# One PSUM tile of eight named banks instead of rings of PSUM tiles

## The chip, the core and the metric

The kernel runs on one core of a Trainium2 chip. A core has five engines that run their own instruction streams: TensorE (PE, matmuls; PEld is its weight load), VectorE (DVE), ScalarE (ACT), GpSimd (POOL) and SyncE (SP), and 16 DMA engines. PE writes its products to PSUM, which has eight banks of 128 partitions x 2 KB; ACT and DVE read them from there. Each engine executes its own stream in order, and an instruction that needs another engine's result waits on a semaphore. The metric is the device time in microseconds (us) of one execution; lower is better.

## The reference

Three stages are chained: causal attention over 2 x 12 heads of 448 rows and 64 columns, and two feed-forward layers on the 896 x 768 result.

```python
scores = scale * q @ k.T ; mask above the diagonal ; attn = softmax(scores) ; x = attn @ v
h = x @ w_in1 ; g = h * cos(h)                                        # 896x768 @ 768x2048
x = g @ w_out1                                                        # 896x2048 @ 2048x768
h = x @ w_in2 ; g = where(h >= 1, h, where(h <= -1, 0, (h + 1)**2 / 4))
out = g @ w_out2
```

## The kernel before

Every float32 operand of a feed-forward product is split into a high and a low part, and a product is three matmuls per chunk of 128: high x high, high x low, low x high. PE therefore has most of the work. The kernel has five parts, one behind the other on PE.

- **Attention** (to 82.6 us in the profile), in the order of the table `STEPS`: S makes scores, M their maxima, E the exponentials, T transposes, C copies them, V multiplies with v, X and Y split the result. Two-bank PSUM tiles come from the pool `ps_s` (two buffers) and one-bank tiles from `ps_t` (four).
- **Stage 1**, `stage_in_plain` (to 200 us): 16 columns blocks of the first hidden layer, each with the gate `h * cos(h)`.
- **Stage 2**, `stage_out(0)` (to 304 us): the first output product as seven products of half-sized matrices instead of eight, four steps t of each (28 in all), and three row blocks d = 0, 1, 2 in each step. A product of one step and one d is six matmuls (L1019). The sums of several of the seven products grow in the same bank (`CHAIN`): ACT or DVE reads the bank between two of them (`keep`, L1045; `result`, L1058 and L1062) and PE goes on adding to it. In the last two steps of some of the seven products the order on PE is: d = 0 of step t-1 and of t, then d = 1 of both, then d = 2 of both.
- **Stage 3**, `stage_in_split` (to 419 us): eight groups g of two hidden blocks. Groups 0 to 5 have seven products of nine matmuls each (L1283), numbered 1 to 7; groups 6 and 7 have plain products (L1382). A group runs 1, then 4 and 3 of the group before, then 6, 2, 7, 5 (group 0: 1, 5, 6, 2, 7). Products 1, 6, 7 and 4 grow in bank x, 2 in bank z, 5 and 3 in bank y. After 1, 6 and 7 ACT copies bank x to SBUF (`keep`, L1295); after 2 DVE makes the result C11 from bank z (L711), after 5 C22 from bank y. Product 7 adds to the bank that the copy behind product 6 reads, so that it has to wait for this copy; this copy is called K6 here.
- **Stage 4**, `stage_out(1)`: as stage 2, for the second layer; `result` also stores to `out`.

In stages 1 to 4 all PSUM tiles hold two banks, [128, 2, 512], from a ring of four (`new_ps`, called by `bank_of` when a name is used first). x and z of a group are the two banks of one tile (`xz`), y has the first bank of another. In stages 2 and 4, d = 0 and d = 1 of a chain are the two banks of one tile (`xa`, `za`, `va`), and the d = 2 of two chains share a tile (`xb`, `zb`).

The order of stages 1 to 4 on each engine is found by a planner (`Plan`, `Steps`). Each step is a `plan.op` with a cost, the parts of buffers that it reads and those that it writes. The planner walks the steps through a model of the engines 300 times with random changes and keeps the best order; PE's own order is fixed by that of the `plan.op` calls. `plan.buf` says which slot a buffer takes; when a slot is taken again, the first writer of each part waits in the plan for all uses of the buffer before. Inside a buffer the planner counts each bank as a part of its own. The semaphores in the program are not the planner's: the tile framework sets them as the instructions are emitted, from the tiles that they read and write.

Of the kernel before, what the change touches and what calls it, by code (L numbers as in the profile page):

```python
# [31 lines left out]

STEPS = """
# [11 lines left out]
Cz10 NbP11 Tx10 Cz9 V9 Cw10 Y8 NcP11 Cy10 Cx10 NaP11 Tz11 Tx11 Tw11 Cz11 V10 D2 Cx11 Cw11 X9 Cy11 V11 Y9 D2 F0 F1 F2 F3  # L45
# [233 lines left out]
def attention_then_two_ffn(  # L279
# [109 lines left out]
    class Pair:  # L389
# [23 lines left out]
        def S(self, g):  # L413


            n = self.n
            if g == "c":
                two = (self, pairs[n + 1])
                for pair in two:
                    pair.s["c"] = ps_t.tile([P, 512], F32, tag="t", name=f"sc{pair.n}")  # L420
# [87 lines left out]
        def T(self, g):  # L508

            n, p = self.n, self.p  # L510
            if g == "x":
                t = ps_s.tile([P, 2, 512], F32, tag="s", name=f"tx{n}")
                moves = [(t[:, j, i * QB : (i + 1) * QB], p[i][:, j, :QB]) for j in range(2) for i in range(FULL)]
                moves += [(t[:, j, 3 * QB :], p[2][:, j, 2 * QB :]) for j in range(2)]
            else:
                t = ps_t.tile([P, 512], F32, tag="t", name=f"t{g}{n}")
# [71 lines left out]
    def ffn_in_part(u, x, b, chunks):  # L588

        if u not in parts:  # L590
            parts[u] = (new_ps(), ready[u], set())
        ps, w, done = parts[u]
        s = slice(b * S, (b + 1) * S)
        for c in chunks:
# [3 lines left out]
            for n, (a, t) in enumerate(((0, 0), (0, 1), (1, 0))):  # L598
                nc.tensor.matmul(  # L599
                    ps[:, b, :S], w[:, a, c * P : (c + 1) * P], x[c][:, t, s],  # L600
# [4 lines left out]
    ps_s = ctx.enter_context(tc.tile_pool(name="ps_s", bufs=2, space=PSUM))  # L605
    ps_m = [ps_s, ps_s]
    made = []

    def new_ps():
        made.append(None)  # L610
        return ps_m[(len(made) - 1) % 4].tile([P, 2, 512], F32, tag="s", name=f"m{len(made)}")

    with ExitStack() as attn:
# [3 lines left out]
        ps_t = attn.enter_context(tc.tile_pool(name="ps_t", bufs=4, space=PSUM))  # L617
# [4 lines left out]
        warm = ps_t.tile([P, 512], F32, tag="t", name="warm")  # L622
# [38 lines left out]
    ps_2 = ctx.enter_context(tc.tile_pool(name="ps_2", bufs=2, space=PSUM))  # L661
    ps_m += [ps_2, ps_2]
# [25 lines left out]
    banks_made = [0]  # L688
# [149 lines left out]
    def stage_in_plain():  # L838

        for u in range(2):  # L840
            ps, w, done = parts[u]
            given(f"w{u}", f"w{u}", w, LETTERS)
            bank_buf(f"h{u}", (0, 1))
            things[f"h{u}"] = ps
# [17 lines left out]
        def batch(f, b, chunks):  # L862
            products(f, tile_of_bank(f)[:, b, :S], slice(b * S, (b + 1) * S), chunks, None, chunks[-1])

        def tile_of_bank(f):
            return bank_of(f"h{f}")

        def flat_products(f, s, chunks):
            products(f, flat(tile_of_bank(f))[:, s], s, chunks, 0, KD - 1)

        def gate(f):
# [6 lines left out]
            hp = [(f"h{f}", 0), (f"h{f}", 1)]  # L878

            def h():  # L880
                ps = tile_of_bank(f)
# [37 lines left out]
        for f in range(0, KF, 2):  # L919
            for u in (f, f + 1):  # L920
# [4 lines left out]
                if u >= 2:  # L925
# [8 lines left out]
                    bank_buf(f"h{u}")  # L934
            if f == 0:
                for u in (0, 1):
                    done = parts[u][2]
                    for b in range(B):
                        left = [c for c in range(KD) if (b, c) not in done]
                        if left:  # L940
                            plan.op(
                                f"P{u}.{b}", "PE", ACC * len(left), partial(batch, u, b, left),
                                [(f"w{u}", p) for p in LETTERS] + [(f"x1{c}", 0) for c in left], [(f"h{u}", b)],
                            )
            else:
                order = list(spans)
                spans.reverse()
                for n, s in enumerate(order):
                    us = KD * 3 * (0.2267 if s.stop - s.start == 512 else 0.1733)
                    half = spans_of.index(s)  # L950
                    for u in (f, f + 1):
# [3 lines left out]
                        for chunks in sets:  # L955
                            plan.op(
                                f"P{u}.{n}.{chunks[-1]}", "PE", us * len(chunks) / KD, partial(flat_products, u, s, chunks),
                                [(f"w{u}", p) for p in LETTERS] + [(f"x1{c}", 0) for c in chunks], [(f"h{u}", half)],
# [5 lines left out]

    def bank(k, name):
        t, i = BANKS[name]
        return bank_of(f"{t}{k}")[:, i, :S]

    BANKS = {
# [3 lines left out]
    }  # L973
# [6 lines left out]
    def stage_out(k, first_products=None, at_split=None, at_result=None):  # L980

        def bank_access(name):
            t, i = BANKS[name]
            return (f"{t}{k}", i)

        def split(t):
# [46 lines left out]
        def keep(name, d):  # L1033
# [3 lines left out]
            if k and name != "p1":  # L1037
                combine(
                    f"{k}{name}.{d}", "DVE", 0.62, lambda: tile_of(kept)[:, d], lambda: bank(k, f"v{d}"),
                    lambda: tile_of("p11")[:, d], ALU.add, [bank_access(f"v{d}"), ("p11", d)], [(kept, d)],  # L1040
# [5 lines left out]
                [bank_access(f"x{d}")], [(kept, d)],  # L1046
            )

        def result(name, d, m, b, chain, old):
# [4 lines left out]
            def make():  # L1054
# [13 lines left out]
                f"{k}{name}.{d}", "DVE", 0.62, make, [bank_access(f"{chain}{d}"), (f"{old}{k}", d)], [(c, d)],  # L1068
# [9 lines left out]
        for t in range(NT7):  # L1078
            p, j = SEQ[k][t]
            if t == 0:  # L1080
                bank_buf(f"xa{k}")
                bank_buf(f"xb{k}")
            if k and (p, j) == (1, 0):
                bank_buf(f"va{k}")
            if t == 2 * NJ:
                bank_buf(f"za{k}")
                bank_buf(f"zb{k}")
# [131 lines left out]
    def group(g):  # L1219
# [37 lines left out]
        def where(n):  # L1257
            return {"x": (f"xz{g}", 0), "z": (f"xz{g}", 1), "y": (f"y{g}", 0)}[PLACE[n]]

        def at(n):  # L1260
            t, s = where(n)
            return bank_of(t)[:, s, :S]

        def product(n):
            if n == 1:
                bank_buf(f"xz{g}")
                bank_buf(f"y{g}")
# [79 lines left out]
        def before(n):  # L1347
# [12 lines left out]
            "C12": ("y", 0, (("w0", 1, "R12"), ("w0", 0, "R22"))), "C11": ("xz", 0, (("w0", 1, "R11"), ("w0", 0, "R21"))),  # L1360
            "C21": ("y", 1, (("w2", 1, "R11"), ("w2", 0, "R21"))), "C22": ("xz", 1, (("w2", 0, "R22"), ("w2", 1, "R12"))),
        }

        def plain_product(name, n):
            if (name, n) == ("C12", 0):
                bank_buf(f"y{g}")
                bank_buf(f"xz{g}")
# [123 lines left out]
```

## Time and profile before

| | |
|---|---|
| median of 3 runs | 528.31 us (528.11 to 528.72) |
| the profiled execution | 528.35 us, of which the span of its instructions is 526.4 us |
| PE busy | 509.2 us, 97% |
| DVE busy | 383.9 us, 73% |
| ACT busy | 344.3 us, 65% |
| POOL busy | 96.2 us, 18% |
| PE's granted clock, mean of the span | 1.00 of full speed |
| last matmul of the span ends | 522.9 us |

Times in the rows are microseconds from the start of the span. A row of a timeline gives the start, the busy time, engine, line, operation, what is written and read, and in brackets the idle time of the engine just before it with what ended it. Matmuls overlap: one of 448 columns starts 0.20 us behind the last and is shown as busy for 0.37, so that what a product takes is read from its start to the start of the next.

### The profile page before, as it was taken

The numbers are of one execution on the slowest core, as the hardware profiler recorded it, in microseconds if no ns is written. First come the engines' busy times: TensorE is split into PE (matmuls) and PEld (weight loads), VectorE is DVE, ScalarE is ACT, GpSimd is POOL, SyncE is SP. The second block draws the span as 40 slices with busy tenths as digits, with TensorE's granted clock in tenths as the row PEclk, the third lists the DMA queues.
The fourth block names the chain that finished last, engine by engine and source line by source line (L and its number), as shares of the span: only waits on it lengthen the run. The fifth ranks groups of instructions, "written<-read, shape, count | busy, mean of one in ns | idle before, by whom it ended". The sixth has DMA issues, their size and how long they took to land.

```text
span 526.4 us, 7606 instructions
## 1 busy us (share of the span) xinstructions
PE 509.2 (97%) x2810; PEld 442.4 (84%) x2810; DVE 383.9 (73%) x534; ACT 344.3 (65%) x604; POOL 96.2 (18%) x157
## 2 busy tenths in 40 slices
PE   8999999999999999999999989999999999999997
PEld 4666778989898899899988978888889999999886
DVE  7879866686666449787578968577777888997652
ACT  5998976677665457655567758776678777745340
POOL 4847560010000102331001111011100012310000
PEclk9999999999999999999999999999999999999999
DMA  8754216799871616895037775454566879970111
GB/s 294 256 163 150 63 39 231 234 291 273 265 226 61 178 61 132 164 189 96 1 120 188 178 189 162 124 134 107 151 215 209 252 220 241 209 148 19 52 54 53
DMA packets 44709, 84.12 MB, mean 160 GB/s; under 512 B 2688, under 2 KB 33408, under 8 KB 44672
## 3 DMA queue, kind: packets, MB, share of 16 engines
q1 hardware_dynamic: 36464, 61.51, 35.6%
q0 software_dynamic: 8064, 21.89, 22.5%
q8 instruction: 22, 0.36, 0.3%
q10 hardware_dynamic: 144, 0.23, 0.1%
q14 instruction: 15, 0.12, 0.1%
HBM read 58.98 MB, written 2.75 MB: 117 GB/s over the span
## 4 chain that ended last, share of the span: by engine, by line
PE 94%; DVE 3%; ACT 1%; issue 1%; DVEq 0%
PE m L1019 39%; PE m L857 20%; PE m L1283 14%; PE m L1382 6%; PE o L552 4%; PE m L599 2%; PE sa L439 2%; PE tx L526 2%; PE sb L439 1%; PE tz L526 1%; PE tw L526 1%; PE warm L624 1%; ACT kept L1295 1%; DVE raw L365 1%; PE sc L424 1%
## 5 line engine op out<-in xcount | busy, mean ns | idle before, releaser
L857 PE MATMUL m<-x,w 128*128 128x384 f32 (+2 forms) x516 | 105.3, 366 | 0.0
L857 PEld LDWEIGHTS m<-x,w 128*128 128x128 f32 x516 | 93.4, 188 | 11.7
L365 DVE SCALAR_TENSOR_TENSOR raw<-raw,top 128x768 uint32<-128x768 uint32 x32 | 30.5, 954 | 9.3 <-ACT top L356 9.1
L356 ACT CAST top<-raw 128x768 f16<-128x768 bf16 x26 | 27.9, 1075 | 8.3 <-DMA raw<-in_moe_w_in 7.7
L1283 PE MATMUL m<-rx,w1g 128*128 128x448 f32 x108 | 24.6, 372 | 3.7 <-ACT kept L1295 3.7
L1283 PE MATMUL m<-rx,w0g 128*128 128x448 f32 x108 | 24.6, 367 | 1.6 <-DVE w0g L726 1.6
L1283 PEld LDWEIGHTS m<-rx,w1g 128*128 128x128 f32 x108 | 19.8, 188 | 7.5 <-ACT kept L1295 6.0
L552 PE MATMUL o<-pT,v 128*64 128x448 f32 (+3 forms) x192 | 23.2, 385 | 0.9 <-ACT pT L543 0.9
L1283 PEld LDWEIGHTS m<-rx,w0g 128*128 128x128 f32 x108 | 20.0, 188 | 4.2 <-DVE w0g L726 2.8
L706 POOL DMA_DIRECT2D raw<-raw x12 | 10.2, 851 | 69.2 <-DVE g1.0.1_3110 L1322 14.6
L506 POOL TENSOR_SCALAR p<-p,ra 128x384 f32<-128x384 f32 (+1 forms) x48 | 22.1, 479 | 3.2 <-ACT p L484 1.2
L552 PEld LDWEIGHTS o<-pT,v 128*64 128x64 f32 x192 | 12.6, 136 | 12.0 <-issue 6.3
L506 POOL TENSOR_SCALAR p<-p,rb 128x256 f32<-128x256 f32 (+1 forms) x32 | 18.1, 577 | 20.4 <-DVE rb L492 15.5
L1283 PE MATMUL m<-rx,w2g 128*128 128x448 f32 x90 | 20.4, 365 | 1.2 <-DVE w2g L726 1.2
L1062 DVE TENSOR_TENSOR c<-m,p 128x448 f32<-128x448 f32 x18 | 10.8, 620 | 13.6 <-PE m L1019 13.5
L1295 ACT COPY kept<-m 128x448 f32<-128x448 f32 x18 | 9.5, 529 | 16.9 <-PE m L1283 14.7
L1283 PEld LDWEIGHTS m<-rx,w2g 128*128 128x128 f32 x90 | 16.8, 188 | 2.9 <-DVE w2g L726 1.6
L484 ACT ACTIVATE p<-sb,nmb 128x256 f32<-128x256 f32 x24 | 11.2, 475 | 7.1 <-DVE nmb L465 4.0
L484 ACT ACTIVATE p<-sa,nma 128x384 f32<-128x384 f32 x24 | 13.8, 583 | 1.4 <-DVE nmd L463 0.7
L726 DVE TENSOR_TENSOR w<-raw,w 128x768 fp32r<-128x768 f32 x14 | 13.3, 950 | 0.9 <-ACT w L717 0.9
L706 POOL DMA_DIRECT2D c<-c x4 | 3.4, 932 | 53.6 <-ACT sw0.23_2750 L717 38.5
L439 PE MATMUL sa<-k,q 64*128 64x384 f32 (+1 forms) x88 | 12.4, 401 | 0.4 <-ACT p L484 0.4
(669 smaller groups left out, 1349.4 us busy)
## 6 DMA issues: line engine op xcount, KB each, us to landing
raw<-in_moe_w_in SPq DMA_DIRECT2D x32, 768.0 KB, 5.0
v<-in_v SPq DMA_DIRECT2D x12, 256.0 KB, 4.0
k<-in_k SPq DMA_DIRECT2D x12, 224.0 KB, 3.8
c<-c POOLq DMA_DIRECT2D x4, 672.0 KB, 6.5
out<-c SPq DMA_DIRECT2D x12, 224.0 KB, 1.9
qr<-in_q SPq DMA_DIRECT2D x11, 224.0 KB, 3.9
raw<-raw POOLq DMA_DIRECT2D x12, 192.0 KB, 4.3
rows0.0_1373<-in_moe_w_out SPq DMA_DIRECT2D x1, 768.0 KB, 4.1
```

Source lines behind the costliest of these rows:

```text
L356: nc.scalar.copy(out=to, in_=what)
L365: nc.vector.scalar_tensor_tensor(out=fl, in0=bits, scalar=13, in1=top, op0=ALU.logical_shift_right, op1=ALU.bitwise_or,)
L439: nc.tensor.matmul(s[:, j, o : o + w], self.q[rows(n, j), i * QB : w], self.k[rows(n, j), :w], start=(o == 0), stop=False,)
L484: nc.scalar.activation(out=o, in_=i, func=AF.Exp, bias=nm[:, m : m + 1], scale=1.0 if n else scale, accum_out=self.r[r][:, c : c + 1],)
L506: e.tensor_scalar(out=p, in0=p, scalar1=r[:, c : c + 1], scalar2=1.0, op0=ALU.mult, op1=ALU.mult)
L526: nc.tensor.transpose(o, i, ident)
L552: nc.tensor.matmul(self.o[heads(j), c * QB : S], self.v[:, j, c, :], self.pT[:, c, j, c * QB :], start=(c == 0), stop=(c == FULL),)
L857: nc.tensor.matmul(o, w[:, a, c * P : (c + 1) * P], x(t, c)[:, s], start=(c == first and n == 0), stop=(c == last and n == 2),)
L1019: nc.tensor.matmul(o, wt[:, a, i * MW + d * P : i * MW + (d + 1) * P], r[:, i], start=(p in (0, k, 2, 4) and j == 0 and i == 0 and n == 0) ...
L1283: nc.tensor.matmul(o, wt[:, l, block, c * P : (c + 1) * P], rt[:, s, x], start=(n in (1, 2, 5) and c == 0 and e == 0), stop=(c == ML - 1 a ...
L1295: f"1K{n}g{g}", "ACT", 0.57, lambda: nc.scalar.copy(out=tile_of("kept")[:, n], in_=at(product_n)),
L1382: nc.tensor.matmul(o, wt[:, l, block, c * P : (c + 1) * P], rt[:, s, x], start=(n == 0 and c == 0 and e == 0), stop=(n == 1 and c == ML - ...
```

## The change

The pools `ps_s`, `ps_t` and `ps_2` go. One tile `psum` of [128, 8, 512] is made once for the whole kernel, and all code takes slices of it.

- In attention the banks are read from two tables: `BANKS_OF_TWO` names the first bank of each pair (0 or 2), `BANKS_OF_ONE` a bank of 4 to 7.
- In stage 1 the hidden blocks take the pairs (0, 1), (2, 3), (4, 5), (6, 7) in turn.
- In stages 2 and 4 each chain and d has one bank (`BANKS`), given to the planner as a buffer of its own; in stage 3 groups take banks 1, 2, 3 and 4, 5, 6 alternately for x, z, y, and the two plain groups 0 to 3 and 4 to 7.
- In `STEPS` two neighbouring words change places (`V9 Cw10` is now `Cw10 V9`); V is PE's, C is ACT's.

```diff
-    ps_s = ctx.enter_context(tc.tile_pool(name="ps_s", bufs=2, space=PSUM))
-    ps_m = [ps_s, ps_s]
+    psum = ctx.enter_context(tc.tile_pool(name="psum", bufs=1, space=PSUM)).tile([P, 8, 512], F32, name="psum")
     made = []
-    def new_ps():
-        made.append(None)
-        return ps_m[(len(made) - 1) % 4].tile([P, 2, 512], F32, tag="s", name=f"m{len(made)}")
+    pairs_of_banks = iter(BANKS_OF_TWO)
+    single_banks = iter(BANKS_OF_ONE)
+    def two_banks():
+        bank = int(next(pairs_of_banks))
+        return psum[:, bank : bank + 2]
+    def one_bank():
+        return psum[:, int(next(single_banks))]
...
-                s = ps_s.tile([P, 2, 512], F32, tag="s", name=f"s{g}{n}")
+                s = two_banks()
...
-            self.o = ps_t.tile([P, 512], F32, tag="t", name=f"o{self.n}")
+            self.o = one_bank()
...
-    def bank_buf(name, parts=()):
-        plan.buf(name, f"ps{banks_made[0] % 4}", parts)
-        things[name] = banks_made[0]
-        banks_made[0] += 1
+    def bank_buf(name, *banks):
+        for n, b in enumerate(banks):
+            plan.buf((name, n), f"ps{b}", (0,) if made else ())
+        things[name] = banks[0]
     def bank_of(name):
-        t = things[name]
-        if isinstance(t, int):
-            assert t == len(made)
-            t = things[name] = new_ps()
-        return t
+        return psum[:, things[name]]
...
+                    b = parts[0][0] % 4
+                    b = (b, 2 - b, 4, 6)[u % 4]
+                    bank_buf(f"h{u}", b, b + 1)
...
-    BANKS = {
-        "v0": ("va", 0), "v1": ("va", 1), "v2": ("xb", 1),
-        "x0": ("xa", 0), "x1": ("xa", 1), "x2": ("xb", 0), "z0": ("za", 0), "z1": ("za", 1), "z2": ("zb", 0),
-        "y0": ("za", 0), "y1": ("za", 1), "y2": ("zb", 1),
-    }
+    BANKS = {
+        "x": (0, 1, 2), "v": (3, 4, 5), "z": ((3, 4, 5), (6, 7, 0)), "y": ((6, 7, 0), (1, 2, 6)),
+    }
...
         def where(n):
-            return {"x": (f"xz{g}", 0), "z": (f"xz{g}", 1), "y": (f"y{g}", 0)}[PLACE[n]]
+            return bank_access(f"{PLACE[n]}{g}")
...
             if n == 1:
-                bank_buf(f"xz{g}")
-                bank_buf(f"y{g}")
+                for letter, b in zip("xzy", ((1, 2, 3), (4, 5, 6))[g % 2]):
+                    bank_buf(f"{letter}{g}", b)
```

No instruction is added or removed. The order on PE, POOL and SP is the same in both programs, and that on ACT and DVE too up to the end of stage 3; in stage 4 the planner moves some 20 instructions of ACT and DVE by a few places. Three places follow, first PE in group 0 of stage 3 before: the end of product 5, product 6 (w1g0 with rx8 and rx1), 2 (w0g0), 7 (w1g0 with rx6 and rx7), and 1 of group 1 (w0g1). m21 is the tile xz of group 0, m22 its y, m23 xz of group 1.

```order
L1283 MATMUL m22_3005<-rx9_2927,w2g0_2963 128x448 x6
L1283 MATMUL m21_2985<-rx8_2942,w1g0_2938 128x448 x6
L1283 MATMUL m21_2985<-rx1_2961,w1g0_2938 128x448 x3
L1283 MATMUL m21_2985<-rx1_2961,w0g0_2902 128x448 x3
L1283 MATMUL m21_2985<-rx2_2995,w0g0_2902 128x448 x6
L1283 MATMUL m21_2985<-rx6_2701,w1g0_2938 128x448 x3
L1283 MATMUL m21_2985<-rx7_2827,w1g0_2938 128x448 x6
L1283 MATMUL m23_3066<-rx14_2839,w0g1_3055 128x448 x6
```

The same place on PE in the changed program:

```order
L1284 MATMUL psum_74<-rx9_2816,w2g0_2852 128x448 x6
L1284 MATMUL psum_74<-rx8_2831,w1g0_2827 128x448 x6
L1284 MATMUL psum_74<-rx1_2850,w1g0_2827 128x448 x3
L1284 MATMUL psum_74<-rx1_2850,w0g0_2791 128x448 x3
L1284 MATMUL psum_74<-rx2_2883,w0g0_2791 128x448 x6
L1284 MATMUL psum_74<-rx6_2590,w1g0_2827 128x448 x3
L1284 MATMUL psum_74<-rx7_2716,w1g0_2827 128x448 x6
L1284 MATMUL psum_74<-rx14_2728,w0g1_2942 128x448 x6
```

Nothing moved; only the tile is another, and with it the banks: products 6 and 7 now write bank 1, 2 writes bank 2, 5 wrote bank 3.

The second place is DVE in stage 4 before, behind the sum ws1.0.0: the sums of g (L711), the decoding of the last weight rows (L365), and the low parts sx and sw of the operands of steps 11 to 14.

```order
L711 TENSOR_TENSOR ws1.0.0_3603<-ws1.0.0_3603 128x768
L711 TENSOR_TENSOR g1.1.0_3258<-g1.1.1_3318 128x896
L365 SCALAR_TENSOR_TENSOR ws1.3.1_4129<-rows1.15_4087,top1_62 128x2x384
L728 SCALAR_TENSOR_TENSOR sx1.12_4168<-g1.0.0_3057,sx1.12_4168 128x896
L726 TENSOR_TENSOR sw1.11_4187<-ws1.3.1_4129,sw1.11_4187 128x768
L728 SCALAR_TENSOR_TENSOR sx1.13_4189<-g1.1.0_3258,sx1.13_4189 128x896
L726 TENSOR_TENSOR sw1.13_4177<-ws1.1.1_3976,sw1.13_4177 128x768
```

The same place on DVE in the changed program:

```order
L717 TENSOR_TENSOR ws1.0.0_3479<-ws1.0.0_3479 128x768
L717 TENSOR_TENSOR ws1.1.0_3591<-ws1.1.0_3591 128x768
L368 SCALAR_TENSOR_TENSOR ws1.3.1_3997<-rows1.15_3957,top1_62 128x2x384
L734 SCALAR_TENSOR_TENSOR sx1.12_4036<-g1.0.0_2944,sx1.12_4036 128x896
L732 TENSOR_TENSOR sw1.11_4055<-ws1.3.1_3997,sw1.11_4055 128x768
L732 TENSOR_TENSOR sw1.13_4046<-ws1.1.1_3846,sw1.13_4046 128x768
L734 SCALAR_TENSOR_TENSOR sx1.13_4057<-g1.1.0_3142,sx1.13_4057 128x896
```

One sum has taken the place of another ahead of sw1.11, and sx1.13 and sw1.13 have changed places.

The third place is DVE at the start of stage 4 before: `g1.3.1<-m35` and `g1.3.0<-m36` are the last gates of stage 3, which read PSUM.

```order
L728 SCALAR_TENSOR_TENSOR sx1.2_3850<-g1.0.0_3057,sx1.2_3850 128x896
L1322 SCALAR_TENSOR_TENSOR g1.3.1_3714<-m35_3734,g1.3.1_3714 128x2x448
L726 TENSOR_TENSOR sw1.2_3862<-ws1.0.0_3603,sw1.2_3862 128x768
L365 SCALAR_TENSOR_TENSOR ws1.3.0_3835<-rows1.7_3791,top1_62 128x2x384
L711 TENSOR_TENSOR g1.0.0_3057<-g1.0.1_3110 128x896
L1322 SCALAR_TENSOR_TENSOR g1.3.0_3747<-m36_3766,g1.3.0_3747 128x2x448
```

The same place on DVE in the changed program:

```order
L734 SCALAR_TENSOR_TENSOR sx1.2_3710<-g1.0.0_2944,sx1.2_3710 128x896
L717 TENSOR_TENSOR g1.1.1_3200<-g1.1.0_3142,g1.1.1_3200 128x896
L717 TENSOR_TENSOR g1.0.0_2944<-g1.0.1_2996 128x896
L732 TENSOR_TENSOR sw1.2_3736<-ws1.0.0_3479,sw1.2_3736 128x768
L368 SCALAR_TENSOR_TENSOR ws1.3.0_3708<-rows1.7_3664,top1_62 128x2x384
L1323 SCALAR_TENSOR_TENSOR g1.3.1_3589<-psum_74,g1.3.1_3589 128x2x448
L1323 SCALAR_TENSOR_TENSOR g1.3.0_3621<-psum_74,g1.3.0_3621 128x2x448
```

The gate g1.3.1 stands four instructions later, and two sums of g stand before it.

## Rows read from the trace of the kernel before

**Rows 1.** The profile's page: busy time by engine, share of the span, instructions

```profile
PE 509.2 (97%) x2810; PEld 442.4 (84%) x2810; DVE 383.9 (73%) x534; ACT 344.3 (65%) x604; POOL 96.2 (18%) x157
```

**Rows 2.** Waits of PE: releaser, total us, times, longest us

```profile
PE m L1283 <- ACT kept L1295: 3.7, 6, 0.6
PE m L1019 <- DVE c L1062: 2.2, 3, 0.7
PE m L1283 <- DVE w0g L726: 1.6, 3, 1.2
PE m L1283 <- DVE w2g L726: 1.2, 1, 1.2
...
PE m L1019 <- DVE c L1058: 0.7, 1, 0.7
PE m L1019 <- ACT p L1045: 0.6, 1, 0.6
PE sa L439 <- ACT p L484: 0.4, 1, 0.4
```

**Rows 3.** Timeline of PE, stage 3, groups 0 and 1

```profile
309.57 1.98 PE L1283 MATMUL m<-rx,w0g 128*128 128x448 f32 x9
312.18 2.10 PE L1283 MATMUL m<-rx,w1g 128*128 128x448 f32 x9 [0.62 <-ACT kept L1295]
314.11 0.57 PE L1283 MATMUL m<-rx,w0g 128*128 128x448 f32 x2
315.86 1.69 PE L1283 MATMUL m<-rx,w0g 128*128 128x448 f32 x7 [1.18 <-DVE w0g L726]
317.39 1.37 PE L1283 MATMUL m<-rx,w2g 128*128 128x448 f32 x6
```

**Rows 4.** Timeline of PE, stage 3, two products without a wait

```profile
327.41 1.98 PE L1283 MATMUL m<-rx,w2g 128*128 128x448 f32 x9
329.23 1.98 PE L1283 MATMUL m<-rx,w0g 128*128 128x448 f32 x9
```

**Rows 5.** Timeline of ACT, stage 3

```profile
311.59 0.53 ACT L1295 COPY kept<-m 128x448 f32<-128x448 f32 x1 [3.48 <-PE m L1283]
312.02 0.84 ACT L717 CAST w0g<-raw 128x768 fp32r<-128x768 f32 x1
...
327.61 0.53 ACT L1295 COPY kept<-m 128x448 f32<-128x448 f32 x1
```

**Rows 6.** Timeline of DVE, stage 3

```profile
314.31 0.62 DVE L711 TENSOR_TENSOR g1.0.0_3057<-m,kept 128x448 f32<-128x448 f32 x1 [4.02 <-PE m L1283]
314.85 0.95 DVE L726 TENSOR_TENSOR w0g<-raw,w0g 128x768 fp32r<-128x768 f32 x1
```

**Rows 7.** Timeline of all engines, stage 2, steps 18 and 19

```profile
268.23 1.36 PE L1019 MATMUL m<-sx0.18_2632,sw0.18_2607 128*128 128x448 f32 x6
...
269.63 0.62 DVE L1058 SCALAR_TENSOR_TENSOR c<-m,p 128x448 f32<-128x448 f32 x1 [0.66 <-PE m L1019]
...
270.31 1.47 PE L1019 MATMUL m<-sx0.19_2657,sw0.19_2634 128*128 128x448 f32 x6 [0.71 <-DVE c L1058]
...
271.61 1.36 PE L1019 MATMUL m<-sx0.18_2632,sw0.18_2607 128*128 128x448 f32 x6
```

**Rows 8.** Timelines of PE and of DVE, stage 2, step 20

```profile
274.01 4.01 PE L1019 MATMUL m<-sx0.20_2683,sw0.20_2659 128*128 128x448 f32 x18
...
275.87 0.62 DVE L1058 SCALAR_TENSOR_TENSOR c<-m,p 128x448 f32<-128x448 f32 x1
```

**Rows 9.** Stretches: length, busy of PE, PEld, DVE, ACT, POOL, granted clock, DMA share, GB/s

```profile
325.47:339.14 13.67, 13.05 (x64) 11.75 (x64) 9.81 (x14) 11.11 (x18) 1.70 (x2) 1.00 0.39 95
...
440.00:476.00 36.00, 35.97 (x180) 33.18 (x179) 33.93 (x40) 21.76 (x30) 8.55 (x10) 1.00 0.84 179
```

**Rows 10.** Timeline of PE, stage 4, step 11

```profile
458.99 4.05 PE L1019 MATMUL m<-sx1.11_4137,sw1.11_4187 128*128 128x448 f32 x18
```

**Rows 11.** Timeline of DVE, stage 4, the low part of the weights of step 11

```profile
458.57 0.95 DVE L726 TENSOR_TENSOR sw1.11_4187<-ws1.3.1_4129,sw1.11_4187 128x768 fp32r<-128x768 f32 x1
```

More of the change, by code (lines that the diff above doesn't have):

```diff
@@ L419, in S @@
                 for pair in two:
-                    pair.s["c"] = ps_t.tile([P, 512], F32, tag="t", name=f"sc{pair.n}")
+                    pair.s["c"] = one_bank()
                 for pair in two:
@@ L511, in T @@
             if g == "x":
-                t = ps_s.tile([P, 2, 512], F32, tag="s", name=f"tx{n}")
+                t = two_banks()
                 moves = [(t[:, j, i * QB : (i + 1) * QB], p[i][:, j, :QB]) for j in range(2) for i in range(FULL)]
@@ L515, in T @@
             else:
-                t = ps_t.tile([P, 512], F32, tag="t", name=f"t{g}{n}")
+                t = one_bank()
                 if g == "z":
@@ L590, in ffn_in_part @@
         if u not in parts:
-            parts[u] = (new_ps(), ready[u], set())
-        ps, w, done = parts[u]
+            bank = int(next(pairs_of_banks))
+            parts[u] = (bank, ready[u], set())
+            made.append(u)
+        bank, w, done = parts[u]
         s = slice(b * S, (b + 1) * S)
@@ L599, in ffn_in_part @@
                 nc.tensor.matmul(
[L600 removed]
+                    psum[:, bank + b, :S], w[:, a, c * P : (c + 1) * P], x[c][:, t, s],
                     start=(first and n == 0), stop=(last and n == 2),
@@ L621, in attention_then_two_ffn @@
         ones = nc.const_aps.tensor(1.0, [P, 512], BF16)
-        warm = ps_t.tile([P, 512], F32, tag="t", name="warm")
+        warm = one_bank()
         for _ in range(8):
@@ L840, in stage_in_plain @@
         for u in range(2):
-            ps, w, done = parts[u]
+            bank, w, done = parts[u]
             given(f"w{u}", f"w{u}", w, LETTERS)
-            bank_buf(f"h{u}", (0, 1))
-            things[f"h{u}"] = ps
+            bank_buf(f"h{u}", bank, bank + 1)
+        made.clear()
         for c in range(KD):
@@ L877, in gate @@
             gp = [(g, (n, i)) for n in range(2)]
-            hp = [(f"h{f}", 0), (f"h{f}", 1)]
+            hp = [bank_access(f"h{f}", n) for n in range(2)]
             def h():
-                ps = tile_of_bank(f)
+                ps = banks_of(f"h{f}")
                 return ps[:, :, :S] if f < 2 else joint(flat(ps))
@@ L942, in stage_in_plain @@
                                 f"P{u}.{b}", "PE", ACC * len(left), partial(batch, u, b, left),
-                                [(f"w{u}", p) for p in LETTERS] + [(f"x1{c}", 0) for c in left], [(f"h{u}", b)],
+                                [(f"w{u}", p) for p in LETTERS] + [(f"x1{c}", 0) for c in left], [bank_access(f"h{u}", b)],
                             )
@@ L957, in stage_in_plain @@
                                 f"P{u}.{n}.{chunks[-1]}", "PE", us * len(chunks) / KD, partial(flat_products, u, s, chunks),
-                                [(f"w{u}", p) for p in LETTERS] + [(f"x1{c}", 0) for c in chunks], [(f"h{u}", half)],
+                                [(f"w{u}", p) for p in LETTERS] + [(f"x1{c}", 0) for c in chunks], [bank_access(f"h{u}", half)],
                             )
@@ L980, in stage_out, with access, banks_for @@
     def stage_out(k, first_products=None, at_split=None, at_result=None):
-        def bank_access(name):
-            t, i = BANKS[name]
-            return (f"{t}{k}", i)
+        def access(name):
+            return bank_access(f"{name}k{k}")
+        def banks_for(letter):
+            banks = BANKS[letter]
+            for d, b in enumerate(banks[k] if letter in "zy" else banks):
+                bank_buf(f"{letter}{d}k{k}", b)
         def split(t):
@@ L1045, in keep @@
                 lambda: nc.scalar.copy(out=tile_of(kept)[:, d], in_=bank(k, f"x{d}")),
-                [bank_access(f"x{d}")], [(kept, d)],
+                [access(f"x{d}")], [(kept, d)],
             )
@@ L1067, in result @@
             plan.op(
-                f"{k}{name}.{d}", "DVE", 0.62, make, [bank_access(f"{chain}{d}"), (f"{old}{k}", d)], [(c, d)],
+                f"{k}{name}.{d}", "DVE", 0.62, make, [access(f"{chain}{d}"), (f"{old}{k}", d)], [(c, d)],
             )
@@ L1079, in stage_out @@
             p, j = SEQ[k][t]
[L1080 to L1087, printed above, removed]
+            for letter, first in (("x", 0), ("v", k), ("z", 2), ("y", 4)):
+                if (p, j) == (first, 0) and (k or letter != "v"):
+                    banks_for(letter)
             if p == 1 and k:
@@ L1359, in group @@
         SUMS = {
-            "C12": ("y", 0, (("w0", 1, "R12"), ("w0", 0, "R22"))), "C11": ("xz", 0, (("w0", 1, "R11"), ("w0", 0, "R21"))),
-            "C21": ("y", 1, (("w2", 1, "R11"), ("w2", 0, "R21"))), "C22": ("xz", 1, (("w2", 0, "R22"), ("w2", 1, "R12"))),
+            "C12": ("one", 0, (("w0", 1, "R12"), ("w0", 0, "R22"))), "C11": ("two", 0, (("w0", 1, "R11"), ("w0", 0, "R21"))),
+            "C21": ("one", 1, (("w2", 1, "R11"), ("w2", 0, "R21"))), "C22": ("two", 1, (("w2", 0, "R22"), ("w2", 1, "R12"))),
         }
@@ L1365, in plain_product @@
             if (name, n) == ("C12", 0):
-                bank_buf(f"y{g}")
-                bank_buf(f"xz{g}")
+                for m, name_of in enumerate(("one", "two")):
+                    bank_buf(f"{name_of}{g}", 4 * (g % 2) + 2 * m, 4 * (g % 2) + 2 * m + 1)
                 fractions("w0", "w0", a, "A")
@@ L1389, in plain_product @@
                 f"1P{name}.{n}g{g}", "PE", 1.82, make, [(w, p) for p in LETTERS] + [(r, (s, p)) for r, s in right for p in LETTERS],
-                [(f"{t}{g}", half_of)],
+                [bank_access(f"{t}{g}", half_of)],
             )
             if n and name in ("C21", "C22"):
-                both = [(f"{t}{g}", 0), (f"{t}{g}", 1)]
-                gate((0, 3) if name == "C21" else (1, 2), (lambda: bank_of(f"{t}{g}")[:, :, :S], both))
+                both = [bank_access(f"{t}{g}", n) for n in range(2)]
+                gate((0, 3) if name == "C21" else (1, 2), (lambda: banks_of(f"{t}{g}")[:, :, :S], both))
         def run_product(*n):
```

32 lines of the change are left out of this document (15 added, 17 removed).

## The prediction

> **What bounds the kernel now.** I read the busy times first [rows 1]: PE is busy for 509.2 us of a span of 526.4, the other engines for three quarters or less. So the end is set by PE's matmuls and by what makes PE stand still, and only 17 us are idle. The list of PE's waits comes next [rows 2]: it says which engine ends PE's idle time, how often, and how long in all. Six of its rows lie in stages 2 to 4 and are touched by the change: 3.7 us for the copy `kept`, 2.2, 0.7 and 0.6 for readers of stages 2 and 4, 1.6 and 1.2 for the low parts of weights, in all 10.0 us in 15 waits. Then I looked at single waits in the timelines of PE and of the engine that PE waits for, to see why that engine is late.
>
> Take the copy K6. In group 0 product 2 begins at 309.57, when product 6 is over, and product 7, which needs the copy of 6, at 312.18 after 0.62 us of idle time [rows 3]; product 2 writes the other bank. The copy began only at 311.59, when PE had finished product 2, and ACT had stood idle for 3.48 us until then [rows 5]. It needs the result of product 6, which was there about 1.8 us sooner. The semaphore that it waits on is that of the last matmul written to the two-bank tile by then, and this is one of product 2. The same is seen with the sum C11 on DVE: it reads the bank of product 2 and begins at 314.31, after 4.02 us of idle time ended by PE [rows 6], which is the end of product 7 and not that of 2. Behind it on DVE stands the low part of w0g, from 314.85 to 315.80, and for that PE waits until 315.86 [rows 3]. In stage 2 the result of d = 0 begins at 269.63, when the six matmuls of d = 1 begun at 268.23 are over, and PE waits for it until 270.31 [rows 7].
>
> So the waits of PE that repeat aren't for slow readers. A reader starts one product late, because two banks share a tile.
>
> **The change part by part.** No matmul, copy, cast or DMA is added or taken away, so that the whole effect is in when instructions may start. In the built program of the change each of the reads that are late in this way has a semaphore value that belongs to the last matmul of its own bank; K6, for one, waits for product 6 and no longer for 2.
>
> What a stall costs is more than its idle time, since PE also starts up more slowly behind it. An undisturbed product takes 327.41 to 329.23, 1.82 us [rows 4]. With K6 products 2 and 7 take 2.61 and 1.93 [rows 3], so 0.79 + 0.11 = 0.90 for 0.62 of idle time. The wait for w0g makes 314.11 to 317.39, 3.28 in place of 1.82, so 1.46 for 1.18. In stage 2 six matmuls take 1.20 at this rate; the two intervals are 2.08 and 1.30 [rows 7], so 0.98 for 0.71. Each time about 0.28 us come on top. All 15 waits: 10.0 + 15 x 0.28 = 14.2 us.
>
> Whether they go depends on what is late next.
> - K6: ACT is idle ahead of it, and a copy of 0.53 us fits into product 2's 1.82. That reading a bank isn't slower while PE writes another is seen at 327.61, where the same copy takes 0.53 beside a running product [rows 4, 5]. The spare time is about 1.2 us. Six K6 waits gone: 6 x 0.90 = 5.4, inside the 14.2.
> - w0g and w2g: C11 can begin at the end of product 2, some 2.7 us sooner than 314.31; the low part of w0g behind it (0.95 us [rows 6]) needs its high part, cast by ACT from 312.02 to 312.86 [rows 5] right behind K6, and this comes forward with K6 by about 1.6 us, to end near 311.2. C11 then ends near 312.2 and the low part near 313.1. PE asked for it at 314.68 (315.86 less the 1.18 of idle time) and will at about 313.8, the 0.90 of K6 sooner. The spare time is 0.7 us, but a low part of rx stands behind it on DVE, so that a rest may stay here, inside the term for new waits below.
> - Stage 2 and 4: the result of 0.62 us now lies beside the 1.20 us of the next half. The spare time is about half a microsecond.
> - Attention: its two-bank tiles are still taken as pairs, but a reader frees each bank of a pair for itself. PE's wait for `p` of 0.4 us [rows 2] and a longer one of the same kind at the start may shorten: between 0 and 0.45 us, and I take 0.3, near the row's own length.
> - New waits, on the other side. With banks named singly a bank is taken again sooner in some places. The tightest is step 20 of stage 2: its third row block starts 12 matmuls or 2.4 us behind 274.01, at about 276.4, and its bank is read by a result on DVE from 275.87 to 276.49 [rows 8]. After the two waits before it go, PE comes earlier by 1 us and DVE by less. Behind this result DVE has the low parts of later steps, which aren't due for 3 us or more, and ACT waits for the result itself. A place like this costs between 0 and the 0.98 of a stage 2 stall; I take 0.2 here and 0.4 for all others together, with up to 2.0 as the far bound (two full stalls).
> - Order in stage 4: g1.3.1 moves behind four other DVE instructions of about 0.85 us each (33.93 us by 40 [rows 9]), so that its two banks come free some 3.4 us later. PE has steps of 18 matmuls, 3.6 us each, on other banks meanwhile, and this is the cover; without it, PE would lose up to those 3.4 us. I take 0. Ahead of sw1.11 one sum of nearly the same length replaces another; between -0.15 and 0.15, I take 0.
> - Swapped words in attention: the streams of PE and ACT each stay as they are, so 0.
>
> Sum: 528.35 (the profiled execution, 0.04 above the median of 528.31; 526.4 of span and 1.9 around it, which stays) - 14.2 - 0.3 + 0.6 = 514.4 us.
>
> The granted clock is 1.00 of full speed in the stretches read, in stage 3 and in stage 4 [rows 9]; with PE less idle I see no reason for it to fall.
>
> **The rivals.**
> A. The feeders become the bound in stage 3. A group of 13.67 us has 11.11 us of ACT and 9.81 of DVE [rows 9]; in 12.77 us (0.90 less) this is 87% and 77%. For it: the four waits for w0g and w2g are waits for DVE's work. Against it: DVE idles for 4.02 us directly ahead of C11 [rows 6], which is a wait for PE and not work. If these waits stay (2.8 + 4 x 0.28 = 3.9), the time is 518.3.
>
> B. Stage 4's operands don't come sooner. From 440 to 476 DVE is busy for 33.93 of 36 us and the DMA engines for 0.84 [rows 9], and at step 11 PE begins at 458.99 [rows 10] while the low part of its weights is ready at 459.52 [rows 11], just before the matmuls that use it. For it: no slack is left there, so that a feed which doesn't move would keep that point at 459 and all that was won before it would be lost. Against it: weights are read into a ring whose places come free as PE moves on, so the feed should move with PE. If it holds, only the two stalls behind it stay won, 2 x 0.98 = 2.0: 526.4.
>
> C. Slower: fixed banks in attention. Before, a score tile alternated between two buffers; the new table of 38 names the same pair twice running 7 times, and another of 49 gives single banks again after two tiles where the ring gave them after four. Each place where the reader of the last tile isn't done when PE comes costs one wait like `sa` for `p`: 0.39 of idle time and 0.28 behind it, 0.67 [rows 2]. It decides from 22 such places (14.7 us) on; with 30 of the 87 tiles the time would be 514.4 + 20.1 = 534.5. For it: attention's products are short, and PE waited for a bank there already. Against it: by the times of before, no reader of a bank ends behind the start of its next writer, and readers of a pair are now let go sooner.
>
> D. The change doesn't do what it says: all slices belong to one tile, and if its waits were kept for the whole tile, every reader would wait for the last matmul of all. That the built program has waits bank by bank speaks against it. A variant: the repeating waits are for a free bank, and nothing of that changes with eight banks before and after. Then the time is 528.3. Against it stands the releaser in [rows 2]: it is the reader of the very bank that product 7 adds to, not one that frees a bank for a new sum.
>
> The Trainium skill ("Perfetto Trace Analysis", section Optimization Strategy) has this variant as a rule: the same gap repeating on the engine that should be saturated can mean that there isn't enough SBUF or PSUM for the next tile. By that rule the six equal gaps would stay, and the trace disagrees so far.
>
> **How the numbers follow.** My forecast, 514.4, has 0.74; A 0.11; B 0.09; C 0.03; D 0.03. The forecast's own range is 513.2 (no new waits, 0.5 less at places that I don't see) to 516 (two small stalls more). The range of 8 in 10 takes in A with a small stall on top: 513.0 to 519.0; B, C and D stay outside. About 0.2%, or 1 us, is what a measurement of this kernel can tell from no change. Forecast, A and B are faster by more than that: 0.94. Within it: D, 0.03. Slower: C, 0.03.
>
> **What would show it.** In the changed profile the list of PE's waits has no row for `kept`, and those for `c`, w0g and w2g in stages 2 to 4 are gone or under 0.3 us each. K6 begins within 0.3 us of product 6's end, while PE is busy with product 2. The stretch of one group is 12.8 us. PE's busy time falls little, by the slow starts only (some 4 us at most), its idle time by about 10. A shows as waits for w0g that stay over 1 us; B as new PE idle time around step 11 of stage 4; C as waits for `p` or `pT` in the first 83 us that are longer than before. The forecast is wrong if less than 12 us are won and no such row says where they went.

## The result, and the profile after

The changed kernel takes 514.13 us, the median of 4 runs (513.51 to 515.48), beside 528.21 for the kernel before (4 runs, 527.84 to 528.72). The ratio is 0.9736, with a 95% interval of 0.9715 to 0.9757. The profiled execution took 514.03 us, 14.32 less than that of before. One of the four runs (515.48 us), and three of the five of the last experiment below, had a mean granted clock of 0.995 to 0.997 in place of 0.999 or 1.000 and took 1 to 2 us longer than the others.

Busy times on the page of the changed kernel, which answer to [rows 1]:

```profile
PE 506.0 (99%) x2810; PEld 445.5 (87%) x2810; DVE 383.6 (75%) x534; ACT 344.3 (67%) x604; POOL 96.2 (19%) x157
```

All waits of PE in the changed kernel, which answer to [rows 2] (releaser, total us, times, longest us):

```profile
PE psum L555 <- ACT pT L546: 0.9, 1, 0.9
PE psum L632 <- PEq L1469: 0.8, 1, 0.8
PE psum L442 <- ACT p L487: 0.6, 1, 0.6
PE psum L529 <- POOL p L509: 0.4, 1, 0.4
```

The first list is nearly the old one, only PE is busy for 3.2 us less, since the slow starts are gone; the work of DVE, ACT and POOL is the same to 0.3 us. In the second list the six rows of stages 2 to 4 are missing. What is left lies in the first 31 us.

How a stall went is seen in group 0 of stage 3. PE in the changed kernel, products 2, 7, 1 of the next group and 4, which answer to [rows 3]:

```profile
306.73 1.98 PE L1284 MATMUL psum<-rx,w0g 128*128 128x448 f32 x9
308.55 2.00 PE L1284 MATMUL psum<-rx,w1g 128*128 128x448 f32 x9
310.39 1.98 PE L1284 MATMUL psum<-rx,w0g 128*128 128x448 f32 x9
312.21 1.37 PE L1284 MATMUL psum<-rx,w2g 128*128 128x448 f32 x6
```

ACT there, K6 and the cast behind it, which answer to [rows 5]:

```profile
306.92 0.53 ACT L1296 COPY kept<-psum 128x448 f32<-128x448 f32 x1 [0.71 <-PE psum L1284]
308.80 0.83 ACT L723 CAST w0g<-raw 128x768 fp32r<-128x768 f32 x1 [1.34 <-PE psum L1284]
```

DVE there, C11 and the low part of w0g, which answer to [rows 6]:

```profile
308.75 0.63 DVE L717 TENSOR_TENSOR g1.0.0_2944<-psum,kept 128x448 f32<-128x448 f32 x1 [0.36 <-PE psum L1284]
309.67 0.96 DVE L732 TENSOR_TENSOR w0g<-raw,w0g 128x768 fp32r<-128x768 f32 x1 [0.29 <-ACT w0g L723]
```

K6 now begins 0.19 us behind the start of product 2, where before it began 2.02 behind it. It is over (at 307.45) 1.1 us before product 7 needs it, and PE has no row with a wait: the products begin 1.82, 1.84 and 1.82 us apart. C11 begins 0.2 us behind the start of product 7, when product 2 is over, and no longer behind the end of 7.

Stage 2, PE and DVE at the place of [rows 7], from the timeline of all engines of the changed kernel:

```profile
267.34 1.36 PE L1026 MATMUL psum<-sx0.18_2521,sw0.18_2496 128*128 128x448 f32 x6
268.00 0.62 DVE L1065 SCALAR_TENSOR_TENSOR c<-psum,p 128x448 f32<-128x448 f32 x1
...
268.54 1.36 PE L1026 MATMUL psum<-sx0.19_2546,sw0.19_2523 128*128 128x448 f32 x6
```

The result on d = 0 now begins beside the first half of d = 1. It ends at 268.62, 0.08 us after the second half has begun: the second half no longer waits for it, and follows 1.20 us behind the first without a pause. The windows of one group of stage 3 and of 440 to 476 us (columns as in [rows 9]):

```profile
319.51:332.31 12.80, 12.80 (x65) 11.83 (x64) 9.12 (x14) 11.24 (x17) 1.70 (x2) 1.00 0.42 110
440.00:476.00 36.00, 36.00 (x180) 33.45 (x179) 31.26 (x37) 18.61 (x23) 5.15 (x6) 1.00 0.51 104
```

The group takes 12.80 us in place of 13.67, and PE is busy in all of it. ACT is at 88% and doesn't decide.

Where the time came from is read by taking the start of the same product in both traces. The shift at the end of each part:

| part | shift at its end | its own share | forecast |
|---|---|---|---|
| attention | +0.03 | 0.0 | -0.3 |
| stage 1 | 0.00 | 0.0 | 0 |
| stage 2 | -2.85 | -2.85 | -2.86 (0.90 + 2 x 0.98) |
| stage 3 | -11.96 | -9.11 | -9.3 (5.4 + 3.9) |
| stage 4 | -14.17 | -2.21 | -1.96 (2 x 0.98) |
| new waits | | none | +0.6 |

The other 0.15 of the 14.32 us lie behind the start of the last matmul.

### The profile page after: what moved, and what is told of

It is laid out like the page before. It is cut to its first block, busy times and chain, and to the rows that moved or that the text cites. A ratio compares the mean times of both kernels' runs of the same rounds, so it can differ in the third digit from the quotient of the medians.

```text
span 512.2 us, 7605 instructions
## 1 busy us (share of the span) xinstructions
PE 506.0 (99%) x2810; PEld 445.5 (87%) x2810; DVE 383.6 (75%) x534; ACT 344.3 (67%) x604; POOL 96.2 (19%) x157
## 4 chain that ended last, share of the span: by engine, by line
PE 97%; DVE 1%; issue 0%; POOL 0%; ACT 0%; POOLq 0%
PE psum L1026 40%; PE psum L863 21%; PE psum L1284 15%; PE psum L1383 6%; PE psum L555 4%; PE psum L529 4%; PE psum L442 4%; PE psum L604 2%; PE psum L632 1%; PE psum L427 1%; DVE nma L466 0%; PE psum L452 0%; PE psum L455 0%; DVE nmc L466 0%; DVE raw L368 0%
## 5 line engine op out<-in xcount | busy, mean ns | idle before, releaser
L863 PE MATMUL psum<-x,w 128*128 128x384 f32 (+2 forms) x516 | 105.3, 366 | 0.0
L863 PEld LDWEIGHTS psum<-x,w 128*128 128x128 f32 x516 | 93.4, 188 | 11.6
L529 PE MATMUL psum<-ident,p 128*128 128x128 f32 x192 | 24.8, 278 | 0.4 <-POOL p L509 0.4
L1284 PE MATMUL psum<-rx,w1g 128*128 128x448 f32 x108 | 24.0, 367 | 0.0
L555 PE MATMUL psum<-pT,v 128*64 128x448 f32 (+3 forms) x192 | 23.2, 385 | 0.9 <-ACT pT L546 0.9
L1284 PE MATMUL psum<-rx,w0g 128*128 128x448 f32 x108 | 23.8, 364 | 0.0
L529 PEld LDWEIGHTS psum<-ident,p 128*128 128x128 f32 x192 | 20.7, 141 | 3.1 <-issue 0.9
L555 PEld LDWEIGHTS psum<-pT,v 128*64 128x64 f32 x192 | 12.6, 136 | 12.0 <-issue 6.4
L1284 PEld LDWEIGHTS psum<-rx,w1g 128*128 128x128 f32 x108 | 20.3, 188 | 1.8
L1284 PEld LDWEIGHTS psum<-rx,w0g 128*128 128x128 f32 x108 | 20.2, 188 | 1.7
L442 PE MATMUL psum<-k,q 64*128 64x256 f32 (+2 forms) x132 | 20.8, 409 | 0.6 <-ACT p L487 0.6
```

The costliest lines, as they stand in the source:

```text
L442: nc.tensor.matmul(s[:, j, o : o + w], self.q[rows(n, j), i * QB : w], self.k[rows(n, j), :w], start=(o == 0), stop=False,)
L555: nc.tensor.matmul(self.o[heads(j), c * QB : S], self.v[:, j, c, :], self.pT[:, c, j, c * QB :], start=(c == 0), stop=(c == FULL),)
L863: nc.tensor.matmul(o, w[:, a, c * P : (c + 1) * P], x(t, c)[:, s], start=(c == first and n == 0), stop=(c == last and n == 2),)
L1284: nc.tensor.matmul(o, wt[:, l, block, c * P : (c + 1) * P], rt[:, s, x], start=(n in (1, 2, 5) and c == 0 and e == 0), stop=(c == ML - 1 a ...
```

## The experiments

Each run stands beside runs of the kernel before on the same chip (528.27 us in the first four, 528.30 in the last four).

**One tile, but the banks of before.** Attention takes the tables of the changed kernel; from stage 1 on the pairs of banks, the planner's buffers and so the order are those of before.

```diff
-    ps_s = ctx.enter_context(tc.tile_pool(name="ps_s", bufs=2, space=PSUM))
+    psum = ctx.enter_context(tc.tile_pool(name="psum", bufs=1, space=PSUM)).tile([P, 8, 512], F32, name="psum")
...
     def new_ps():
-        made.append(None)
-        return ps_m[(len(made) - 1) % 4].tile([P, 2, 512], F32, tag="s", name=f"m{len(made)}")
+        made.append(int(next(pairs_of_banks, -1)))
+        b = made[-1]
+        if b < 0:
+            b = (made[0], 2 - made[0], 4, 6)[(len(made) - 1) % 4]
+        return psum[:, b : b + 2]
```

> One tile of eight banks for the whole kernel, but stages 1 to 4 keep the pairs of banks and the order of before (x and z of a group, d = 0 and d = 1 of a chain side by side); attention takes the tables of the changed kernel. Theory (a reader waits for the last matmul written to its tile, where the tile has two banks, and with the tile of eight banks for its own bank only): all 15 waits go, 514.0 to 514.6 us, PE idle time 2.7 us, no wait for kept, w0g, w2g or c. Rival (the new choice of banks and the new order of stage 4 do it): the waits stay, 527.5 to 528.3 us.

Measured: 514.21 us (514.12 to 514.57), ratio 0.9734 (0.9719 to 0.9748). PE's waits in it:

```profile
PE psum L555 <- ACT pT L546: 0.9, 1, 0.9
PE psum L637 <- PEq L1479: 0.8, 1, 0.8
PE psum L442 <- ACT p L487: 0.5, 1, 0.5
PE psum L529 <- POOL p L509: 0.3, 1, 0.3
```

So the tile of eight banks by itself brings the whole gain. Which banks the sums have, that they are named singly, and the moved instructions of stage 4 bring nothing that can be measured: in this run the order on ACT and DVE is that of before in every stage.

**The bank z beside y.** One word of the kernel before is changed; all tiles still have two banks.

```diff
-            return {"x": (f"xz{g}", 0), "z": (f"xz{g}", 1), "y": (f"y{g}", 0)}[PLACE[n]]
+            return {"x": (f"xz{g}", 0), "z": (f"y{g}", 1), "y": (f"y{g}", 0)}[PLACE[n]]
```

> The kernel before with one word changed: in stage 3 the bank z is the second bank of y's tile and not of x's. Copies of x then have no matmul of product 2 in their tile. Theory: the six waits for kept go (6 x 0.90) and with them those for w0g and w2g (3.9), those of stages 2 and 4 stay (5 x 0.98): 518.7 to 519.4 us. Rival (the waits for w0g and w2g are for DVE's load and not for its late start): only 5.4 us go, 522.9 us.

Measured: 519.06 us (518.61 to 519.89), ratio 0.9826 (0.9811 to 0.9841). The waits of PE that this kernel has in stages 2 to 4:

```profile
PE m L1019 <- DVE c L1062: 2.1, 3, 0.7
...
PE m L1019 <- DVE c L1058: 0.7, 1, 0.7
PE m L1019 <- ACT p L1045: 0.6, 1, 0.6
```

The waits for `kept`, w0g and w2g are gone, the five of stages 2 and 4 have stayed. So those for w0g and w2g were not DVE's load; they came of C11's late start. Stage 3 by itself gave 9.1 us between the same two products (the shift goes from -0.29 to -9.39), as in the changed kernel.

**The same banks in smaller tiles.** The banks and the order of the changed kernel, but the eight banks are four tiles of two, and then two tiles of four. Only the tile that a slice belongs to differs. The edit for four tiles; that for two has 4 in place of 2, and `range(2)`:

```diff
-    psum = ctx.enter_context(tc.tile_pool(name="psum", bufs=1, space=PSUM)).tile([P, 8, 512], F32, name="psum")
+    ps_pool = ctx.enter_context(tc.tile_pool(name="psum", bufs=1, space=PSUM))
+    ps_tiles = [ps_pool.tile([P, 2, 512], F32, tag=f"b{i}", name=f"b{i}_") for i in range(4)]
...
+                return ps_tiles[i // 2][:, i % 2 : i % 2 + key[1].stop - i]
+            return ps_tiles[key[1] // 2][(key[0], key[1] % 2) + tuple(key[2:])]
```

> The changed kernel with the same banks and the same order on every engine, but the eight banks are four tiles of two (0 and 1, 2 and 3, 4 and 5, 6 and 7). Theory: the readers wait for the other bank of their tile again, where two neighbours are in use together: K6 in groups 1, 3 and 5 (x and z in banks 4 and 5), 3 x 0.90; C11 of groups 3 and 5 and with it w0g and w2g, up to 2.5; three waits in stage 2, 3 x 0.98; attention 0 to 5: 519.7 to 527 us, with waits for kept in just three groups. Rival (it is the banks and their order): 514.1 us.

> As the run before, with two tiles of four banks (0 to 3, 4 to 7). Theory: nearly every reader of PSUM waits for the last matmul of any of four banks; x, z and y of a group lie in one tile or nearly so, and results come one to two products late: all six K6 waits (5.4), w0g and w2g with 1.8 or more each, stages 2 and 4 three to six waits of 1 us or more: over 530 us, slower than the kernel before. Rival: 514.1 us.

Measured: 536.85 us (535.38 to 538.88) with four tiles, ratio 1.0152 (1.0134 to 1.0169), and 629.74 us (627.97 to 632.79) with two, ratio 1.1925 (1.1882 to 1.1968). Of the waits with four tiles, those of stages 2 and 3 and four of attention:

```profile
PE b__75 L442 <- ACT p L487: 3.3, 3, 2.4
PE b__76 L555 <- ACT pT L546: 1.9, 1, 1.9
...
PE b__76 L1294 <- ACT kept L1306: 1.9, 3, 0.6
PE b__77 L555 <- ACT pT L546: 1.7, 1, 1.7
...
PE b__76 L529 <- ACT pT L546: 1.3, 1, 1.3
PE b__77 L1294 <- DVE w2g L742: 1.2, 1, 1.2
...
PE b__77 L1036 <- DVE c L1079: 0.7, 1, 0.7
PE b__77 L1036 <- DVE c L1075: 0.7, 1, 0.7
PE b__74 L1036 <- ACT p L1062: 0.6, 1, 0.6
...
PE b__74 L1294 <- DVE w0g L742: 0.2, 1, 0.2
```

The waits for `kept` are three, in the groups whose x and z share a tile, and the three of stage 2 are there too. In the profiled execution (538.88 us) the part behind attention is 7.7 us longer than in the changed kernel (the shift goes from 17.1 to 24.8), near the 8.1 that the terms of the expectation give (2.7 + 2.5 + 2.9). So the tile is the cause, shown from both sides. These tiles are made once and never given back, as the one of eight is, so that the ring of before is not needed for the waits. The total was missed: attention costs 17.1 us more and not 0 to 5. Banks 4 to 7 were tiles of one bank in the attention of before and share two tiles here (`b__76` and `b__77`); at the products with v (L555) PE now waits twice for a late copy, 1.9 and 1.7 us, where before it waited once, for 0.9. That this sharing is behind all of the new waits in attention was not shown by itself. Over attention, to 99.4 us, PE is idle for 14.4 us in place of 2.7, 11.8 more. Most of the other 5.3 are due to the clock. Windows of that run, in its first 44 us (columns as in [rows 9]):

```profile
10.00:12.00 2.00, 1.05 (x10) 0.31 (x8) 0.82 (x3) 0.00 (x0) 0.06 (x1) 1.00 0.85 252
12.00:14.00 2.00, 0.47 (x4) 0.40 (x6) 1.97 (x6) 1.94 (x9) 0.00 (x0) 1.00 1.05 357
...
16.00:18.00 2.00, 1.79 (x10) 1.00 (x8) 1.93 (x8) 2.00 (x9) 1.57 (x4) 0.50 0.53 187
18.00:20.00 2.00, 2.00 (x18) 1.49 (x15) 0.92 (x2) 1.29 (x6) 1.17 (x2) 0.70 0.17 32
...
15.80:19.20 3.40, 3.19 (x21) 1.75 (x18) 2.25 (x9) 3.40 (x13) 2.73 (x6) 0.50 0.39 137
36.30:43.10 6.80, 6.10 (x36) 4.25 (x33) 3.84 (x7) 3.02 (x12) 1.09 (x3) 0.50 0.08 14
```

PE stood idle for 2.5 of the 4 us from 10 to 14. Behind that the granted clock is 0.50, the lower level of 1.2 GHz, from 15.8 to 19.2 us, though PE has work again. Behind the wait of 1.9 us that ends at 34.97 it is 0.50 once more, from 36.3 to 43.1 us. In these two stretches PE falls 1.2 and 3.7 us further behind the same products of the changed kernel; 0.2 and 0.7 of that are idle time, so that about 3.9 of the 5.3 us go with the lower clock. The other 1.4 were not divided further. Over the attention of this run the clock is 0.95 in the mean, where the changed kernel has 1.00.

With two tiles nearly every reader is late: PE is busy for 54.0 of the first 83 us, at a mean clock of 0.80. Of the 117 us by which its span is longer than that of the changed kernel, 80 lie in attention, for which the expectation had no term, so that its 530 us were the right side and far too low a figure.

**A longer copy, in both kernels.** K6 is run twice and four times in place of once in the changed kernel, and twice in the one before. The edit for twice:

```diff
+            def copy():
+                for _ in range(2 if product_n == 6 else 1):
+                    nc.scalar.copy(out=tile_of("kept")[:, n], in_=at(product_n))
...
-                f"1K{n}g{g}", "ACT", 0.57, lambda: nc.scalar.copy(out=tile_of("kept")[:, n], in_=at(product_n)),
+                f"1K{n}g{g}", "ACT", 0.57, copy,
```

> The changed kernel, with K6 (the copy behind product 6) run twice in each of the six groups, 0.43 us more of ACT each. Theory (K6 lies beside product 2 with 0.9 to 1.1 us to spare): nothing, 514.1 to 514.6 us. Rival (ACT, busy for 11.1 us of a group of 12.8, has become the bound of stage 3): 6 x 0.43 more, 516.7 us.

> The same with K6 four times, 1.29 us more each. Theory: the last copy ends 0.2 to 0.4 us behind the end of product 2, so that PE waits 0.26 to 0.39 us in each group and loses 0.28 more behind each wait: 517.0 to 518.2 us, and the waits for kept are six again. Rival (ACT is the bound): 6 x 1.29, 521.9 us.

> The kernel before, with K6 twice: 0.43 us more of ACT in each group. Theory (there K6 starts when product 2 is over, and PE waits for its end): each of the six waits grows by 0.43, 530.9 us. Rival (PE's wait is not for the copy itself): 528.3 us.

Measured: 514.08 us (513.46 to 514.61), 518.43 us (518.10 to 518.84) and 532.16 us (531.57 to 532.32). PE and ACT in group 0 of the changed kernel with four copies, first PE:

```profile
306.37 1.98 PE L1284 MATMUL psum<-rx,w0g 128*128 128x448 f32 x9
308.85 2.11 PE L1284 MATMUL psum<-rx,w1g 128*128 128x448 f32 x9 [0.50 <-ACT kept L1297]
310.80 1.98 PE L1284 MATMUL psum<-rx,w0g 128*128 128x448 f32 x9
```

then ACT:

```profile
306.57 2.23 ACT L1297 COPY kept<-psum 128x448 f32<-128x448 f32 x4 [1.09 <-PE psum L1284]
```

The same second copy costs nothing in the changed kernel and 3.9 us in the one before, where nothing lies beside it. So K6 was on the path before and is off it now, and ACT's load is not the bound of stage 3. The copies come 0.57 us apart and not 0.43: (2.23 - 0.53) / 3. In the trace each copy behind the first waits on the semaphore that ACT's own instructions raise, with 0.03 us of idle time before it (all four write the same buffer); the 0.43 was read from K6 and a cast into another buffer. With that the four copies end at 308.80, and product 7 begins at 308.85 instead of 308.19; this group loses 0.77 us (0.66 + 0.11 on the next product), where 0.54 to 0.67 were expected, so that 518.43 lies just above the range. The step of 0.57 for one copy more in the kernel before is 3.4 of its 3.9 us too; the rest is 0.2 in the first 10 us and what runs differ by.

**The longest wait that is left.** In the table of attention one word is moved, so that a copy stands ahead of a cast that waits for DVE.

```diff
-... Tx2 Ma4 D0 D0 Rb4
-Q7 Sc6 Cw3 NcP4 ...
+... Tx2 Ma4 Cw3 D0 D0 Rb4
+Q7 Sc6 NcP4 ...
```

> The changed kernel; one word in the table of attention stands earlier, so that ACT copies the transposed p of pair 3 (L546, at 29.43 us) ahead of the cast of w (L381, at 28.69), which waits for DVE. PE's longest remaining wait, 0.87 us at 30.06 for this copy, should go, with 0.28 behind it: theory 513.0 us, and the cast of w is late by no more than 0.5 us, which nobody waits for. Rival (the next bank or operand is late in the same place): 513.8 to 514.3 us.

Measured: 515.1 us over 5 runs (513.43 to 515.28), ratio 0.9745 (0.973 to 0.9759). PE's waits in it:

```profile
PE psum L632 <- PEq L1469: 0.8, 1, 0.8
PE psum L442 <- ACT p L487: 0.4, 1, 0.4
PE psum L529 <- POOL p L509: 0.4, 1, 0.4
PE psum L442 <- ACT pT L538: 0.3, 1, 0.3
```

The wait of 0.86 us at 30.06 is gone, and the product is 1.08 us sooner; 0.39 are lost again at the next bank, which waits for another copy, and from there to the end this profiled execution is 0.65 ahead of that of the changed kernel. In the times it isn't seen: the forecast was 513.0, the median is 515.1, and the shortest run, 513.43, is as short as the shortest of the changed kernel (513.51). This experiment is inconclusive, and is not called an improvement.

## Why the prediction was right

The time was forecast at 514.4 and came to 514.13; the main terms hold one by one.

- **What PE waited for.** The reading was that readers are late because two banks share a tile. The lists of waits, and the runs with one tile, with z beside y and with smaller tiles show it. The price of a stall, idle time and 0.28 more, fits: at 268 us of stage 2 the same products are 0.98 us closer (the shift goes from -0.89 to -1.87), a group of stage 3 with its K6 is 0.87 shorter (13.67 to 12.80), where 0.90 were forecast. Over the 15 places what is won is 0.23 to 0.29 us more than the gap, be it 0.22 or 1.18 us long.
- **K6 fits beside product 2.** It has 1.0 to 1.1 us to spare in the six groups, of the 1.2 that were forecast; a second copy costs nothing, and a fourth brings the wait back.
- **w0g and w2g.** They go, but with less room than I worked out. In group 0 K6 came 4.67 us sooner (311.59 to 306.92), the cast of w0g behind it only 3.22: it begins at 308.80 and waits for PE, with product 2's last matmul, the last reader of the old w0g, just over. The low part ends at 310.63. The third matmul of product 1, which needs it, begins at about 310.79 (310.39 and two steps of 0.20), and so 0.16 us were to spare and not 0.7. At the three other places it is 0.6 to 1.5 us.
- **The results of stages 2 and 4.** I gave them half a microsecond to spare beside the next half. None was needed: the result begun at 268.00 ends 0.08 us behind the start of the half that waited for it before, and PE goes on. With a bank of its own each d is free of the result on the other.
- **New waits, +0.6.** There are none. At step 20 of stage 2 DVE's result moved from 275.87 to 274.00, by the same 1.87 us as PE; I had taken that DVE would come forward by less. DVE waits for PE too (there through a cast on ACT), and so both moved together.
- **Attention, -0.3.** Nothing of it is left at its end (+0.03). The first wait there is shorter, 0.64 in place of 0.99, but the first products of two runs of the same attention already differ by as much: in the run with z beside y, whose attention is that of before, PE is 0.44 us ahead at its end. The term was too small to tell. These two terms were wrong by 0.6 and 0.3 with opposite signs, which by luck made the forecast 0.3 better than its parts.
- **Stage 4.** The feed moved with PE, and the order there cost nothing: the shift stays at -11.96 from the start of the stage to step 11, past the place where g1.3.1 now stands later. There the low part of sw1.11 came sooner by more than PE did, which is worth 0.2 us (the shift goes from -11.96 to -12.16). The kernel with the order of before in stage 4 takes the same time, 514.21.

Of the rivals, A and B have no row in the profile, C is refuted by attention's unchanged end, and D by the lists of waits. The 528.3 us given for D were too low for its first form: with just four banks guarded as one the kernel takes 629.74. The Trainium skill's rule behind the variant of D ("Perfetto Trace Analysis", section Optimization Strategy, on consistent bubbles) doesn't apply here: the kernel has the same eight banks and all 15 gaps are gone. Another rule fits the runs better: the Trainium skill ("PSUM — Partial Sum Buffer", section PSUM bank collisions raise a hardware error) says to guard PSUM by bank and quadrant, in the simple version by the bank, and not by address. The trace agrees that a guard by the bank is enough for two banks: K6 takes 0.53 us beside product 2 in the next bank, as it does alone.

What stays open: that a slice of the tile of eight banks is waited for by its bank and one of a tile of two or four by the tile is seen in the runs; why the framework makes this difference was not looked into, and tiles of one bank each were not tried.

## What to carry to other kernels

When an engine that should never stop has short gaps of the same length, look at when the instruction that it waits for began, and what ended that one's own idle time: a reader that waits for a product that it doesn't read points to a tile that is guarded as a whole. Changing one word that puts two buffers in different tiles is a cheap test of it. Before counting on a gap's going, look for what is next: here the next reason stood 0.16 us behind the first in one place (w0g in group 0), and 1.0 us or more in others (K6).

## What the hardware did that I had not expected

- In the run with four tiles PE's clock was 0.50 of full speed for 3.4 us after PE had stood idle for 2.5 of 4 us, and for 6.8 us after it had stood idle for 1.9 of 4, while it had work. So a stall in a stretch with several of them costs more than its own gap: 17.1 us for 11.8 of idle time. In the kernel before, whose longest wait is 1.2 us, the clock is 1.00; in the one with two tiles of four banks the mean over the whole span is 0.957.
